# Reordering the tokens while x is split, so that the first product of a fused attention and feed-forward kernel reads plain columns

## The chip, the cores and the metric

The kernel runs on one core of one Trainium2 chip. The metric is the device time of one execution in microseconds; the time of a kernel is the median over several executions. Engines are named as the profile names them: PE is TensorE (PEld its weight loads), DVE is VectorE, ACT is ScalarE, POOL is GpSimd, SP is the engine that issues the DMAs.

## The reference

Windowed attention with 32 global tokens, then a feed-forward block. There are 8 batches with 8 heads, 512 local and 32 global tokens, head size 64; d_model is 512 and d_ff 2048.

```python
s_ll = np.where(abs(i - j) <= 32, scale * q_l @ k_l.T, -1e9)
a_l = softmax(concat[scale * q_l @ k_g.T, s_ll])
out_l = a_l @ concat[v_g, v_l]
out_g = softmax(scale * q_g @ concat[k_g, k_l].T) @ concat[v_g, v_l]
x = concat[out_g, out_l].transpose(0, 2, 1, 3).reshape(4352, 512)
h = x @ w_in
g = h * erf(softplus(h))
return g @ w_out
```

## The kernel before, in words

**Order.** No engine's order is written by hand. Every step is an operation with a key, a guessed duration on each engine that may run it (`add({"DVE": ..., "ACT": ...}, key, ...)`), and the tiles that it reads and writes. `Program.schedule` runs through these guesses once, at build time, and fixes which engine takes which operation and in which order each engine's queue stands. On the chip each queue runs in that order and waits by semaphores. So a changed guess can move other operations too.

**Attention** (`attention`, `attention_global`). For each batch and head: scores `s` (PE), mask and maximum `sm`, `mx` (DVE), exponential (ACT), transposes `t` (PE) copied to `pt`, values `o` (PE), normalised to `xn`, turned to `xT` by a DVE transpose of 32x32 blocks, and stored to a scratch tensor `xsc` in DRAM by four DMAs. The global tokens go the same way through `ga`, `gb`, `pg`, `gt`, `go`, `xg`, `gx` to `xsg`.

**x in DRAM.** Row d of `xsc[b]` holds one feature of 512 tokens. Because the DVE transposes blocks, the tokens of a row stand in the order (a, t, q): a is which of four blocks of 32 within a tile of 128 tokens, t which tile, q the token within the block. Token order would be (t, a, q).

**Feed-forward block.** The 4352 rows of x are nine chunks: eight with 512 local tokens of one batch, and chunk 8 with the 256 global tokens. The weights don't fit at once, so there are two passes (`ps` 0 and 1) over half of d_ff each, and pass 0 leaves its part of the output in DRAM (`part`). Pass 0 is interleaved with the attention of later batches. All products are in fp32r with three terms: a value is split into a high part (`xh`, `winh`, `gh`, `wouth`) and a low part (`xl`, ...), and high·high, low·high and high·low are summed.

- `load_x` loads a chunk's x in two halves `rx` of 128 x 1024 (two slices j of 512 tokens), copies each half to `xh` (which rounds it to fp32r) and subtracts to get `xl`.
- `unit` makes one 128-row slice of h for a chunk: `mm1` issues 4 x 3 = 12 matmuls with `winh` or `winl` as stationary and `xh` or `xl` as moving operand. A chunk of 512 has 8 units in each pass, chunk 8 has 4 of two rows (12 matmuls of 256 columns for each row).
- `gate` computes softplus and erf on ACT, and splits g to `gh`, `gl`.
- `project` issues groups of 6 matmuls `op` (stationary `gh` or `gl`, moving `wouth` or `woutl`, 512 plain columns).

In `mm1` the moving operand of chunks 0 to 7 is read in token order out of the (a, t, q) order:

```python
xh, xl = (t.ap[:, j, :] for t in (HI, LO))
if c < B:
    xh, xl = (t.rearrange("p (a t q) -> p t a q", a=4, q=WB) for t in (xh, xl))
```

That is 16 runs of 32 columns. Chunk 8 reads 256 plain columns. The tiles `xh` and `xl` have three buffers each, so that the second half of the next chunk takes the buffer that the first half of the present one leaves.

Line 278 of the profile is the helper `pe` that records every matmul, 279 the transposes on PE, 280 ACT, 282 DMA, 290 DVE and POOL: groups are told apart by their tiles.

Of the kernel before, what the change touches and what calls it, by code (L numbers as in the profile page):

```python
# [11 lines left out]
F32 = mybir.dt.float32  # L12
# [5 lines left out]
ALU = mybir.AluOpType  # L18
AX = mybir.AxisListType

P = 128
WB = 32
# [23 lines left out]
    "va_0_7": "oh0",  # L46
}
NORMAL = 1.125 * 2.0**-15
SET_EXP = "exp_and_others"
SET_SOFTPLUS = "softplus"  # L50
SET_ERF = "sigmoid_and_others"
# [29 lines left out]
class Program:  # L81
# [9 lines left out]
    def add(self, ways, key, fn, reads=(), writes=(), moved=0.0, heat=0):  # L91


        op = Op()
        op.ways, op.fn, op.key, op.seq, op.moved = ways, fn, key, len(self.ops), moved
        op.heat = heat
        op.outs, op.at, op.new, op.eng = [], 0.0, [], None
        op.slack = max(SLACK.get(e, 0.0) for e in ways)
        op.port = not any(b.pool in self.psum for b in reads)
        deps = set()  # L100
        for b in reads:
            deps.update(b.writers)
        for b in writes:
            deps.update(b.writers)
            deps.update(b.readers)
            if b not in self.allocated:
                self.allocated.add(b)
                if b.pool is not None:
                    op.new.append(b)
        op.bufs = [b for b in dict.fromkeys([*reads, *writes]) if b.pool is not None]  # L110
        for b in op.bufs:
            b.users += 1
        for b in writes:
            b.writers, b.readers = [op], []
        for b in reads:
            if b not in writes:
                b.readers.append(op)
        op.waits = len(deps)
        for d in deps:
            d.outs.append(op)  # L120
        self.ops.append(op)
        return op
# [117 lines left out]
def kernel(  # L240
# [12 lines left out]
    B, NPAIR, _, SQ = qT.shape  # L253
# [22 lines left out]
    add = prog.add  # L276
# [16 lines left out]
    vec = {"DVE": dve, "POOL": pool}  # L293

    def copy(e, dst, src):
        if e == "ACT":
            act(dst, src, AF.Copy)
        else:
            dve.tensor_copy(dst, src)

    def fixed(t):
        b = Buf(None, None, None, None, None)
        b.ap = t
        return b

    def load(key, dst, src, kbytes, deps=(), also=()):
        add({"SP": 0.06}, key, lambda: dma(dst.ap, src), reads=deps, writes=[dst, *also], moved=kbytes)
# [13 lines left out]
    TAB = fixed(None)  # L321
    add({"ACT": 1.3}, -99, lambda: table(SET_EXP), writes=[TAB])

# [256 lines left out]
    def mbuf(shape, dtype, name, tag, bufs):  # L580
        return Buf(mp, shape, dtype, name, tag, bufs)

    def load_w(key, src, name, HI, LO, i, deps):
# [20 lines left out]
        def normal():  # L604
            a = TOP.ap.bitcast(F32)
            dve.scalar_tensor_tensor(
                a, HI.ap[:, i, :].bitcast(F32), NORMAL, a, op0=ALU.is_gt, op1=ALU.mult
            )
# [23 lines left out]
    def load_x(ps, c, key):  # L632

        n = SL if c < B else B * SG
        X = []
        for i in range(2):
            RAW = mbuf([P, 2 * SL], F32, f"rx_{ps}_{c}_{i}", "raw", 3)
            HI = mbuf([P, 2 * SL], F32R, f"xh_{ps}_{c}_{i}", "xh", 3)
            LO = mbuf([P, 2 * SL], F32R, f"xl_{ps}_{c}_{i}", "xl", 3)
            for t in (RAW, HI, LO):  # L640
                t.view = [P, 2, n]
            src = (xsc[c] if c < B else xsg)[2 * P * i : 2 * P * i + 2 * P, :]
            deps = [XSC[c, p] for p in range(2 * i, 2 * i + 2)] if c < B else XSG
            load(key + 0.1 * i, RAW, src.rearrange("(k p) t -> p k t", p=P), 2.048 * n / 2, deps)
            k = key + 0.1 * i + STEP * 2
            add({"DVE": 0.002 * n - 0.2, "ACT": 0.0018 * n + 0.2}, k, lambda e, HI=HI, RAW=RAW: copy(e, HI.ap, RAW.ap), [RAW], [HI])
            add({"POOL": 0.0048 * n + 0.3, "DVE": 0.0026 * n + 0.15},
                k,
                lambda e, HI=HI, LO=LO, RAW=RAW: vec[e].tensor_tensor(
                    LO.ap, RAW.ap, HI.ap.bitcast(F32), ALU.subtract  # L650
                ),
                [RAW, HI],
                [LO],
            )
            X += [(HI, LO, j) for j in range(2)]
        return X

    def unit(ps, c, v, X, key):

        nm = f"{ps}_{c}_{v}"  # L660
        n = SL if c < B else B * SG
        HP = Buf(ps_h, [P, SL // n, n], F32, f"h_{nm}", "h", 2)

        def mm1(a, r):
            o = HP.ap[:, r, :]
            WH, WL = W["in", ps, a // 2]
            for k, (HI, LO, j) in enumerate(X):
                c0 = 256 * (k % 2) + P * (a % 2)
                wh, wl = (t.ap[:, k // 2, c0 : c0 + P] for t in (WH, WL))
                xh, xl = (t.ap[:, j, :] for t in (HI, LO))  # L670
                if c < B:
                    xh, xl = (t.rearrange("p (a t q) -> p t a q", a=4, q=WB) for t in (xh, xl))
                pe(o, wh, xh, start=(k == 0), stop=False)
                pe(o, wh, xl, start=False, stop=False)
                pe(o, wl, xh, start=False, stop=(k == NKT - 1))

        rows = [v] if c < B else [2 * v, 2 * v + 1]
        xs = [t for HI, LO, _ in X[::2] for t in (HI, LO)]
        for r, a in enumerate(rows):
            add({"PE": 0.00533 * n}, key + 0.01 * r, lambda a=a, r=r: mm1(a, r), [*xs, *W["in", ps, a // 2]], [HP], heat=12 * n)  # L680
        Hb = mbuf([P, SL], F32, f"hs_{nm}", "hs", 7)
        SPb = mbuf([P, SL], F32, f"sp_{nm}", "sp", 7)
        add({"ACT": 0.58, "DVE": 0.69}, key, lambda e: copy(e, Hb.ap, HP.ap.rearrange("p a t -> p (a t)")), [HP], [Hb])
        return Hb, SPb

    def gate(ps, c, us, key, first):
        def erf():
# [6 lines left out]
            if ps == 0:  # L694
                table(SET_EXP)

# [109 lines left out]
    for ps in range(2):  # L806
        for c in range(NCHT):
            s = NU * (17 * ps + 2 * c)
            n = NV if c < B else NU
            if ps == 1 and c == 0:  # L810
                for i in range(5, 2 * NU):
                    load_late(i)
            X = load_x(ps, c, s - XLEAD)
            us = [unit(ps, c, v, X, s + v) for v in range(n)]
            last = ps == 1 and c == NCHT - 1
            G = []
            for a, z in ((0, 2), (2, 3), (3, 4)) if last else [(i, i + 4) for i in range(0, n, 4)]:
                G += gate(ps, c, us[a:z], s + z + GOFF, a)
            project(ps, c, G, s + 4 + POFF)
# [76 lines left out]
```

## Time and profile before

| what | value |
|---|---|
| median of 3 runs | 985.0 us (984.0 to 987.04) |
| the profiled execution, its own time | 984.08 us |
| its span on the core, granted PE clock | 982.4 us, 0.988 |
| PE busy | 950.2 us (97%), 9068 matmuls |
| DVE, ACT, POOL busy | 548.2, 540.3, 303.6 us |
| DMA | 127.62 MB, mean 130 GB/s |
| PE share of the chain that ended last | 88% |

The span runs from the first to the last instruction. Busy is the time in which an engine had at least one instruction in flight; matmuls overlap, so the rate of PE is read from the starts of neighbouring matmuls and not from the length of one. The granted clock is 1.00 where the PE ran at 2.4 GHz, and 0.5 where it ran at 1.2 GHz.

### The profile page before, as it was taken

The numbers are of one execution on the slowest core, as the hardware profiler recorded it, in microseconds if no ns is written. First come the engines' busy times: TensorE is split into PE (matmuls) and PEld (weight loads), VectorE is DVE, ScalarE is ACT, GpSimd is POOL, SyncE is SP. The second block draws the span as 40 slices with busy tenths as digits, with TensorE's granted clock in tenths as the row PEclk, the third lists the DMA queues.
The fourth block names the chain that finished last, engine by engine and source line by source line (L and its number), as shares of the span: only waits on it lengthen the run. The fifth ranks groups of instructions, "written<-read, shape, count | busy, mean of one in ns | idle before, by whom it ended". The sixth has DMA issues, their size and how long they took to land.

```text
span 982.4 us, 22140 instructions
## 1 busy us (share of the span) xinstructions
PE 950.2 (97%) x9068; PEld 758.5 (77%) x9068; DVE 548.2 (56%) x1344; ACT 540.3 (55%) x869; POOL 303.6 (31%) x211
## 2 busy tenths in 40 slices
PE   8977899999999999999999999999999999999996
PEld 6756677777778777777888888888888888888895
DVE  5788899584662756855696398323424242333332
ACT  4354586473565645655586756455655544445670
POOL 2232375242342213321153246322213221212140
PEclk9989999999999999999999999999999999999998
DMA  9779876484360662742442334112304040311203
GB/s 356 213 245 288 251 232 189 126 279 121 95 217 0 210 209 61 227 124 82 141 150 65 107 108 129 65 47 83 95 35 129 1 129 0 107 45 43 85 2 107
DMA packets 79740, 127.62 MB, mean 130 GB/s; under 512 B 12184, under 2 KB 37784, under 8 KB 79640
## 3 DMA queue, kind: packets, MB, share of 16 engines
q1 hardware_dynamic: 79640, 126.22, 41.3%
q8 instruction: 71, 1.16, 0.5%
q14 instruction: 29, 0.24, 0.1%
HBM read 99.45 MB, written 26.74 MB: 128 GB/s over the span
## 4 chain that ended last, share of the span: by engine, by line
PE 88%; DVE 7%; DMA 2%; issue 1%; SPq 0%; ACT 0%; DVEq 0%; ACTq 0%
PE op L278 38%; PE h L278 36%; PE s L278 3%; PE o L278 3%; PE t L279 2%; PE spare L278 2%; DVE top_out L290 2%; DVE sm L290 2%; PE go L278 1%; PE ga L278 1%; DMA xsc<-xT 1%; DVE top_in L290 1%; PE gt L279 1%; DVE xT L290 1%; DVE gh L290 0%
## 5 line engine op out<-in xcount | busy, mean ns | idle before, releaser
L278 PE MATMUL h<-xh,winh 128*128 128x512 f32 (+1 forms) x576 | 225.1, 391 | 0.4 <-DVE hs L290 0.4
L278 PE MATMUL h<-xl,winh 128*128 128x512 f32 (+1 forms) x576 | 221.1, 384 | 0.0
L278 PE MATMUL h<-xh,winl 128*128 128x512 f32 (+1 forms) x576 | 221.0, 384 | 0.0
L278 PE MATMUL op<-wouth,gh 128*128 128x512 f32 x544 | 217.3, 399 | 0.5 <-DVE mx L290 0.5
L278 PE MATMUL op<-wouth,gl 128*128 128x512 f32 x544 | 213.2, 392 | 0.0
L278 PE MATMUL op<-woutl,gh 128*128 128x512 f32 x544 | 212.9, 391 | 0.0
L290 POOL TENSOR_TENSOR sp<-sp,hs 128x512 f32<-128x512 f32 x73 | 107.4, 1492 | 212.2 <-ACT sp L280 212.2
L280 ACT ACTIVATE hs<-h 128x512 f32<-128x512 f32 x86 | 51.3, 596 | 162.7 <-PE h L278 162.5
L290 DVE TENSOR_TENSOR gl<-sp,gh 128x512 fp32r<-128x512 f32 x77 | 73.5, 959 | 107.9 <-ACT gh L280 107.0
L280 ACT ACTIVATE gh<-sp 128x512 fp32r<-128x512 f32 x122 | 73.9, 626 | 99.8 <-PE op L278 78.8
L278 PEld LDWEIGHTS h<-xh,winh 128*128 128x128 f32 x576 | 108.7, 189 | 24.9 <-issue 0.8
L278 PEld LDWEIGHTS h<-xh,winl 128*128 128x128 f32 x576 | 108.7, 189 | 23.4
L290 POOL TENSOR_TENSOR gl<-sp,gh 128x512 fp32r<-128x512 f32 x59 | 87.4, 1485 | 126.5 <-ACT gh L280 97.7
L278 PEld LDWEIGHTS h<-xl,winh 128*128 128x128 f32 x576 | 108.8, 189 | 21.5
L278 PEld LDWEIGHTS op<-wouth,gh 128*128 128x128 f32 x544 | 102.2, 188 | 24.1 <-issue 1.7
L278 PEld LDWEIGHTS op<-wouth,gl 128*128 128x128 f32 x544 | 102.1, 188 | 22.1
L278 PEld LDWEIGHTS op<-woutl,gh 128*128 128x128 f32 x544 | 102.3, 188 | 20.6
L281 ACT ACT_TABLE_LOAD x90 | 115.5, 1283 | 2.3 <-PEq L883 0.7
L290 DVE COPY hs<-h 128x512 f32<-128x512 f32 x50 | 34.3, 686 | 108.3 <-PE h L278 108.2
L290 POOL TENSOR_TENSOR sm<-sm,mx 128x512 f32<-128x512 f32 x36 | 40.5, 1130 | 162.8 <-DVE mx L290 98.4
L290 DVE TENSOR_TENSOR sp<-sp,hs 128x512 f32<-128x512 f32 x63 | 65.3, 1058 | 29.9 <-ACT sp L280 29.9
L280 ACT ACTIVATE sp<-sp 128x512 f32<-128x512 f32 x136 | 74.8, 620 | 0.4
(75 smaller groups left out, 1172.5 us busy)
## 6 DMA issues: line engine op xcount, KB each, us to landing
vb<-in_vB_dram SPq DMA_DIRECT2D x64, 325.0 KB, 3.7
rx<-xsc SPq DMA_DIRECT2D x32, 512.0 KB, 4.6
va<-in_vA_dram SPq DMA_DIRECT2D x64, 195.0 KB, 3.6
k<-in_kE_dram SPq DMA_DIRECT2D x32, 384.0 KB, 5.8
q<-in_qT_dram SPq DMA_DIRECT2D x32, 272.0 KB, 4.6
part<-os SPq DMA_DIRECT2D x34, 256.0 KB, 2.1
pr<-part SPq DMA_DIRECT2D x34, 256.0 KB, 3.9
out_dram<-os SPq DMA_DIRECT2D x34, 256.0 KB, 3.9
```

What stands on the lines that cost most here:

```text
L278: pe = lambda n, *a, **k: pinned(nc.tensor.matmul(n, *a, **k))
L279: tr = lambda *a, **k: pinned(nc.tensor.transpose(*a, **k))
L280: act = lambda *a, **k: pinned(nc.scalar.activation(*a, **k))
L281: table = lambda name: pinned(nc.scalar.preload_act_table_set(name))
L290: return lambda *a, **k: pinned(f(*a, **k))
```

## The change

The copy that makes `xh` and the subtraction that makes `xl` now read `rx` in token order and write plain columns. As a half holds two slices j, each of the two operations becomes two instructions of 128 x 512 (chunk 8: 128 x 256, and nothing is reordered there). `mm1` then reads plain columns for every chunk. The guesses for the copy are changed as well. `STRAIGHT` is False, so all of chunks 0 to 7 are reordered.

```diff
-            add({"DVE": 0.002 * n - 0.2, "ACT": 0.0018 * n + 0.2}, k, lambda e, HI=HI, RAW=RAW: copy(e, HI.ap, RAW.ap), [RAW], [HI])
-            add({"POOL": 0.0048 * n + 0.3, "DVE": 0.0026 * n + 0.15},
-                k,
-                lambda e, HI=HI, LO=LO, RAW=RAW: vec[e].tensor_tensor(
-                    LO.ap, RAW.ap, HI.ap.bitcast(F32), ALU.subtract
-                ),
...
+            def in_order(t, j, moved=c < B and not (c == 0 and STRAIGHT)):
+
+                t = t.ap[:, j, :]
+                return t.rearrange("p (a t q) -> p t a q", a=4, q=WB) if moved else t.rearrange("p (t a q) -> p t a q", a=4, t=t.shape[1] // P)
+
+            def split_hi(e, HI=HI, RAW=RAW):
+                for j in range(2):
+                    copy(e, in_order(HI, j, False), in_order(RAW, j))
+
+            def split_lo(e, HI=HI, LO=LO, RAW=RAW):
+                for j in range(2):
+                    hi, lo = (in_order(t, j, False) for t in (HI, LO))
+                    vec[e].tensor_tensor(lo, in_order(RAW, j), hi.bitcast(F32), ALU.subtract)
+
+            add({"DVE": 0.0014 * n, "ACT": 0.0022 * n + 0.1}, k, split_hi, [RAW], [HI])
+            add({"POOL": 0.0048 * n + 0.3, "DVE": 0.0026 * n + 0.15}, k, split_lo, [RAW, HI], [LO])
...
-                xh, xl = (t.ap[:, j, :] for t in (HI, LO))
-                if c < B:
-                    xh, xl = (t.rearrange("p (a t q) -> p t a q", a=4, q=WB) for t in (xh, xl))
+                xh, xl = HI.ap[:, j, :], LO.ap[:, j, :]
```

The number of PE instructions stays what it was. Which engine takes which half moves: before, ACT makes 20 of the 36 `xh` and POOL 16 of the 36 `xl` (DVE the rest); now it is ACT 18 and POOL 20.

DVE, in batch 2's attention, at the second half of x of chunk 0 (names are tile_pass_chunk_half, or tile_batch_head, with a running number). Before:

```order
L290 RECIPROCAL rs_1_5_1698<-rs_1_5_1698 128x4
L290 CAST xh_0_0_1_1707<-rx_0_0_1_1587 128x1024
L290 TENSOR_TENSOR xn_1_4_1589<-o_1_5_1668,rs_1_5_1698 128x4x64
L290 TENSOR_TENSOR xl_0_0_1_1731<-rx_0_0_1_1587,xh_0_0_1_1707 128x1024
L290 STREAM_TRANSPOSE xT_1_5_1747<-xn_1_4_1589 128x512
```

Now:

```order
L291 RECIPROCAL rs_1_5_1700<-rs_1_5_1700 128x4
L291 CAST xh_0_0_1_1709<-rx_0_0_1_1589 128x512 x2
L291 TENSOR_TENSOR xn_1_4_1591<-o_1_5_1670,rs_1_5_1700 128x4x64
L291 TENSOR_TENSOR xl_0_0_1_1734<-rx_0_0_1_1589,xh_0_0_1_1709 128x512 x2
L291 STREAM_TRANSPOSE xT_1_5_1751<-xn_1_4_1591 128x512
```

Nothing moved here; each of the two operations became two instructions.

PE, further on in the attention of batch 2, at the first place at which its order differs. Before (of the eight rows of scores `s_2_4` the last two stand here, of the twelve of unit `h_0_0_3` the first):

```order
L278 MATMUL s_2_4_0_1995<-k_2_4_1753,q_2_4_1751 32x128 x4
L278 MATMUL s_2_4_1_1996<-k_2_4_1753,q_2_4_1751 32x128 x4
L279 MATMUL t_2_2_2050<-cs_75,sm_2_2_1905 128x128 x4
L279 MATMUL t_2_3_2059<-cs_75,sm_2_3_1912 128x128 x4
L278 MATMUL h_0_0_3_2068<-xh_0_0_0_1050,winh_0_1_142 128x512
```

Now (again the last two rows of the `s_2_4`, and the first of `s_2_6`, of `o_2_2` and of `h_0_0_3`):

```order
L280 MATMUL t_2_2_2008<-cs_75,sm_2_2_1906 128x128 x4
...
L279 MATMUL s_2_4_0_2026<-k_2_4_1757,q_2_4_1755 32x128 x4
L279 MATMUL s_2_4_1_2027<-k_2_4_1757,q_2_4_1755 32x128 x4
L279 MATMUL gx_2_0_2068<-cs_75,xg_2_0_2024 128x64
L280 MATMUL t_2_3_2071<-cs_75,sm_2_3_1917 128x128 x4
L279 MATMUL s_2_6_0_2079<-k_2_6_1761,q_2_6_1759 32x128 x4
...
L279 MATMUL o_2_2_2118<-va_2_2_1698,pt_2_2_2009 32x65
...
L279 MATMUL h_0_0_3_2135<-xh_0_0_0_1050,winh_0_1_142 128x512
```

The transposes `t_2_2` moved ahead of the scores, `gx_2_0` ahead of `t_2_3`, and unit `h_0_0_3` behind `s_2_6` and the first values `o_2_2`. From here to the end of attention PE's order differs in many places. Counted over the whole program, PE's order changed from attention work to an `h` or `op` product 90 times before and 83 times now, and an `op` group followed an `h` of a chunk of 512 directly 52 times before and 50 times now.

## Rows read from the trace of the kernel before

**Rows 1.** Busy time by stretch, whole core: us, busy (count) by engine, clock, DMA.

```profile
89.50:166.50 77.00, 70.41 (x1162) 54.69 (x1158) 71.94 (x226) 50.41 (x97) 40.06 (x28) 0.98 0.79 245
166.50:973.10 806.60, 806.59 (x6220) 647.55 (x6220) 410.41 (x864) 450.33 (x692) 237.91 (x159) 1.00 0.34 104
```

**Rows 2.** The same stretches, instructions that touch tile h alone (no POOL column).

```profile
89.50:166.50 77.00, 37.57 (x144) 26.93 (x144) 2.70 (x4) 4.53 (x8) 0.98 0.79 245
166.50:973.10 806.60, 363.85 (x1584) 283.56 (x1584) 31.58 (x46) 46.76 (x79) 1.00 0.34 104
```

**Rows 3.** Waits of PE, 89.5 to 166.5 and behind: us, times, longest.

```profile
PE t L279 <- DVE xg L290: 4.2, 1, 4.2
...
PE op L278 <- DVE mx L290: 0.5, 1, 0.5
```

**Rows 4.** The chain that ended last, pieces: start us, us, what.

```profile
698.92 5.48 PE op L278 x24
...
712.68 8.40 PE h L278 x36
...
935.76 7.19 PE h L278 x60
```

**Rows 5.** Timeline of PE, 700 to 712: start us, us of one, instruction.

```profile
702.88 0.39 PE L278 MATMUL op<-wouth,gh 128*128 128x512 f32 x1
...
704.24 0.40 PE L278 MATMUL h<-xh,winh 128*128 128x512 f32 x1
...
707.03 0.39 PE L278 MATMUL op<-wouth,gh 128*128 128x512 f32 x1
...
708.42 0.39 PE L278 MATMUL op<-wouth,gh 128*128 128x512 f32 x1
```

**Rows 6.** Groups by form on PE: count, busy us, mean ns, idle before.

```profile
L278 PE MATMUL h<-xh,winl 128*128 128x256 f32 x64 | 18.1, 283 | 0.0
```

**Rows 7.** Tile xh: engine, operation, count, ns min/median/max, first and last start, forms.

```profile
L280 ACT ACTIVATE xh<-rx x20: 623/1058/1064, 52.3 to 927.5; 128x1024 fp32r<-128x1024 f32 x18, 128x512 fp32r<-128x512 f32 x2
L290 DVE TENSOR_TENSOR xl<-rx,xh x20: 682/1218/2322, 88.1 to 930.1; 128x1024 fp32r<-128x1024 f32 x19, 128x512 fp32r<-128x512 f32 x1
L290 POOL TENSOR_TENSOR xl<-rx,xh x16: 1288/2393/3252, 54.0 to 886.3; 128x1024 fp32r<-128x1024 f32 x13, 128x512 fp32r<-128x512 f32 x3
L290 DVE CAST xh<-rx x16: 417/694/1604, 87.2 to 885.8; 128x1024 fp32r<-128x1024 f32 x14, 128x512 fp32r<-128x512 f32 x2
```

**Rows 8.** Timeline of DVE, 84 to 130, two instructions.

```profile
88.08 1.22 DVE L290 TENSOR_TENSOR xl<-rx,xh 128x1024 fp32r<-128x1024 f32 x1
...
106.14 2.34 DVE L290 TENSOR_SCALAR gh<-cs,gr 128x2 f32<-128x2 f32 x1
```

**Rows 9.** Timelines of POOL and of PE, around 106 us; in brackets the idle time before.

```profile
106.12 2.34 POOL L290 TENSOR_TENSOR xl<-rx,xh 128x1024 fp32r<-128x1024 f32 x1 [1.69 <-ACT xh L280]
...
108.95 1.09 PE L279 MATMUL t<-cs,sm 128*128 128x128 f32 x4 [4.21 <-DVE xg L290]
```

**Rows 10.** Timeline of PE around one group of attention work between two h units.

```profile
226.10 0.40 PE L278 MATMUL h<-xh,winl 128*128 128x512 f32 x1
226.43 0.24 PE L278 MATMUL o<-va,pt 128*32 128x65 f32 x1
...
227.47 0.50 PE L278 MATMUL h<-xh,winh 128*128 128x512 f32 x1
227.81 0.40 PE L278 MATMUL h<-xl,winh 128*128 128x512 f32 x1
```

**Rows 11.** Timelines of ACT, POOL and PE at the change of chunk in pass 1.

```profile
750.15 1.06 ACT L280 ACTIVATE xh<-rx 128x1024 fp32r<-128x1024 f32 x1 [1.61 <-PE h L278]
...
751.29 2.40 POOL L290 TENSOR_TENSOR xl<-rx,xh 128x1024 fp32r<-128x1024 f32 x1 [10.57 <-ACT xh L280]
...
756.84 0.40 PE L278 MATMUL h<-xh,winh 128*128 128x512 f32 x1
```

**Rows 12.** The chain that ended last, 85 to 200 us: the longest piece that isn't PE's.

```profile
94.69 5.67 DMA xsc<-xT
```

More of the change, by code (lines that the diff above doesn't have):

```diff
@@ L48 @@
 NORMAL = 1.125 * 2.0**-15
+STRAIGHT = False
 SET_EXP = "exp_and_others"
@@ L645, in load_x @@
             k = key + 0.1 * i + STEP * 2
-            add({"DVE": 0.002 * n - 0.2, "ACT": 0.0018 * n + 0.2}, k, lambda e, HI=HI, RAW=RAW: copy(e, HI.ap, RAW.ap), [RAW], [HI])
-            add({"POOL": 0.0048 * n + 0.3, "DVE": 0.0026 * n + 0.15},
-                k,
-                lambda e, HI=HI, LO=LO, RAW=RAW: vec[e].tensor_tensor(
-                    LO.ap, RAW.ap, HI.ap.bitcast(F32), ALU.subtract
-                ),
-                [RAW, HI],
-                [LO],
-            )
+            def in_order(t, j, moved=c < B and not (c == 0 and STRAIGHT)):
[10 more added lines that the diff above has]
+            add({"POOL": 0.0048 * n + 0.3, "DVE": 0.0026 * n + 0.15}, k, split_lo, [RAW, HI], [LO])
             X += [(HI, LO, j) for j in range(2)]
```

## The prediction

> **What bounds the kernel now.** I read the busy time by stretch first. Between 166.5 and 973.1 us PE has work in flight for 806.59 of 806.60 us at a clock of 1.00 (2.4 GHz) [rows 1]. The list of PE's waits agrees: behind 89.5 us it has one long wait, 4.2 us for `xg`, and the last one, 0.5 us, ends the early stage [rows 3]. So from 166.5 us on the end is set by how fast PE goes through its queue, and by nothing else: a nanosecond taken from a matmul there is a nanosecond off the time. Ahead of it, from 89.5 to 166.5 us, DVE is the fuller engine (71.94 of 77 us busy, PE 70.41 [rows 1]); there PE's gain can be lost in waits for DVE. Ahead of 89.5 us no `h` product runs.
>
> Then I read PE's rate, from the starts of matmuls and not from their lengths. In the chain, 36 `h` matmuls of 512 columns take 8.40 us, 0.2333 us each, and 24 `op` matmuls of the same size 5.48 us, 0.2283 us each [rows 4]. The timeline splits the `op` number. The six `op` ahead of an `h` unit take 704.24 − 702.88 = 1.36 us, 0.2267 us each; the six right behind an `h` unit take 708.42 − 707.03 = 1.39 us [rows 5]. The reader is to see two things: the steady gap is 6.7 ns a matmul, and the first groups of `op` behind `h` lose about 0.04 us (5.48 − 4 x 1.36, for four groups of six).
>
> Is the gap due to the order of the columns, or to something else in `h`, its tiles, its weights, its PSUM buffers? Chunk 8 is the control: same code, same pools, but 256 plain columns, 7.19 us for 60, 0.1198 us each [rows 4]. At 2.4 GHz, 256 columns are 0.1067 us and 512 are 0.2133 us. What a matmul takes beyond its columns is then 13.1 ns for plain `h`, 13.4 ns for plain `op`, and 20.0 ns for reordered `h`. The extra goes with the order: 6.7 ns is 16 periods of 2.4 GHz, and the pattern has 16 runs.
>
> **The change part by part.**
>
> *The 512-column `h` matmuls (A).* Behind 166.5 us there are 1584 `h` matmuls [rows 2], of which 3 x 64 = 192 have 256 columns [rows 6]: 1392 x 6.67 ns = 9.3 us. Between 89.5 and 166.5 us there are 144 [rows 2], worth 0.96 us. PE waits for DVE there, so I count half, 0.5 us; the bounds are 0 and 0.96.
>
> *The slow `op` behind `h` (B).* If `h` streams at the rate of `op`, the change of rate is gone, and 52 x 0.04 = 2.1 us with it. Nothing in the trace shows a plain 512-column `h` ahead of `op`, so the bounds are 0 and 2.1 us. I take 2.1, since within a run of `op` a change of group costs nothing.
>
> *Groups of attention work between products (C).* The reshuffled order has 83 of them where there were 90. One costs 227.81 − 227.47 − 0.23 = 0.11 us on the way back to `h`, and 226.43 − 226.10 − 0.23 = 0.10 us on the way out [rows 10]. Seven fewer are worth 0.7 (one way) to 1.5 us; I take 1.1 us.
>
> *The split on the early path (D).* The first `h` can start only when the DVE's `xl` of 88.08 us, 1.22 us long, is done [rows 8]. In two instructions of 512 it takes 2 x 0.682 = 1.36 us, and the copy 2 x 0.417 = 0.83 in place of 0.694 us [rows 7]: +0.3 us, all counted. The trace has no DVE copy with a reordered source. If it ran at the pace of the subtraction (0.682 us for 512) it would add 0.5 us more. It can't be less than nothing: there are as many elements and more instructions. I take 0.3, as the pattern only breaks into 16 runs. The Trainium skill (VectorE: DVE Perf Modes, Mode 2×_2P) lets an fp32 copy in SBUF keep two elements per cycle when the outermost dimension is even, here 4; no row here shows it for this pattern, and by it D would be the 0.3 taken.
>
> *The splits behind 166.5 us.* Two instructions cost more on every engine: ACT 1.06 to 2 x 0.623 = 1.25 us, POOL 2.39 to 2 x 1.288 = 2.58 us [rows 7]. What hides them is that PE has other work. The tightest place is the second half of a chunk: its `xh` waits for a buffer that the present chunk leaves, at 750.15 us; its `xl` is done at 751.29 + 2.40 = 753.69, and `h` reads it from 756.84 [rows 11]. The margin is 3.15 us, and 0.4 us of it goes. Cost: nothing. Without the cover it would be 0.4 us for each of 16 chunks, 6.4 us in all.
>
> *The early order (E).* Around 104.7 us PE waits 4.2 us: `xg` stands on DVE behind a 128x2 operation that took 2.34 us, and this ended together with a POOL subtraction of `xl` that began at the same time and took as long [rows 8, 9]. In the new order `gx_2_0`, `t_2_3`, `s_2_6` and part of `o_2_2` stand ahead of `h_0_0_3` on PE, so less product work can start early behind that wait; on the other hand the POOL operation is now two halves, and the DVE may get in between. The place can gain the whole stall or get a second one. A stall's price is 4.2 us plus the lower clock behind it, (1 − 0.98) x 77 = 1.5 us [rows 1]: 5.7 us. I take 0 and keep ±5.7 for the range.
>
> **Sum.** The profiled execution took 984.1 us, its span 982.4. 984.1 − 9.3 − 0.5 − 2.1 − 1.1 + 0.3 = 971.4 us. It was 0.9 us below the median of 985.0, so for a median I say **972.3 us**. No change that can be measured is within 0.3%, 982.0 to 988.0 us.
>
> **The rivals.**
>
> 1. *Plain columns are no faster for `h`.* The 0.2333 us would belong to something that `h` has at 512 columns alone. Against it stands chunk 8's 13.1 ns beyond its columns; for it, that no 512-column plain `h` is in the trace. A and B fall: 984.1 − 1.1 + 0.3 + 0.9 = 984.2 us, no change. It decides if the starts of `h` stay 0.233 us apart. Two pages speak for it. The Trainium skill (SBUF — State Buffer, Door 1: The DMA port swizzle) has reads lose only where they go to a new line of 16 bytes, and runs of 32 fp32 go to as many lines as plain columns do; and (TensorE: Matmul & The Clock Gate, Step-by-step: what each phase is for) it takes one column of the moving operand per cycle whatever the pattern. By these rules the reordered read was free all along. The trace disagrees so far: 20.0 against 13.4 ns.
>
> 2. *One more early stall.* The mechanism of E comes out on the bad side once: 972.3 + 5.7 = 978.0 us, still faster. For it speaks that DVE is 93% busy from 89.5 to 166.5 us [rows 1] and gets longer instructions; against it, that the assignment in the first chunk is unchanged.
>
> 3. *Slower: DVE's queue blocks on the store of `xT`.* `xT` has one buffer, and a transpose had to wait for a store that held the chain for 5.67 us [rows 12]; what PE needs next then stands behind it in DVE's queue. The new order moves these transposes among other work. Each time that PE has nothing else meanwhile costs about 5.7 us, by the same account as a stall in E. With 12.7 us gained and 3.0 us to be seen, it takes three such places between 105 and 420 us: 972.3 + 17.1 = 989.4 us. Against it: PE has not one such wait behind 166.5 us now, with DVE busy for half of the time there (410.41 of 806.60 us [rows 1]).
>
> **Chances.** Forecast 0.80, rival 1 0.08, rival 2 0.07, rival 3 0.05. So faster by over 0.3%: 0.87, within 0.3%: 0.08, slower: 0.05. The range: the low end is the forecast with the present stall gone, 972.3 − 5.7, about 967. The high end is rival 2 with B at zero, 978.0 + 2.1, about 980. That leaves out rivals 1 and 3 and the ends of the others, under 2 in 10.
>
> **What would show it.** In the profile after: starts of `h` matmuls 0.227 us apart in pass 1, and a chain with 36 of them in about 8.16 us; 24 `op` behind `h` in 5.44 us in place of 5.48; PE busy without a gap from about 165 us to its last matmul; `xl` on POOL in pieces of 1.3 us, and of 0.68 us on DVE; the idle time of PE between 90 and 166 us still about 6.6 us. The prediction is wrong if `h` keeps 0.233 us, if the list of PE's waits has new entries of several microseconds, or if the `xl` of a chunk's second half ends after the first `h` of that chunk could start.

## The result, and the profile after

The change made the kernel faster: a median of 976.3 us (973.44 to 977.58, 5 runs) against 984.0 us (981.61 to 987.04, 5 runs) for the kernel before. The ratio is 0.9917, with a 95% interval of 0.989 to 0.9945, which is −8.1 us. The forecast was 972.3 us in a range of 967 to 980. The profiled execution took 973.44 us, the fastest of the five, with a span of 971.6 us at a granted clock of 0.988.

The rate of PE first. These are pieces of the chain that ended last, of the changed kernel (start us, us, what); they answer to [rows 4].

```profile
725.05 5.44 PE op L279 x24
...
749.53 8.16 PE h L279 x36
...
925.08 7.19 PE h L279 x60
```

36 `h` now take 8.16 us, 0.2267 us each, and the 24 `op` behind an `h` unit take 5.44 us, so the gap in rate and the slow first `op` are both gone. Chunk 8, which was not touched, keeps its 7.19 us.

Then the busy time by stretch (us, then busy us and count for PE, PEld, DVE, ACT and POOL, then clock and DMA), which answers to [rows 1]:

```profile
88.00:165.00 77.00, 70.29 (x1147) 54.19 (x1140) 74.71 (x225) 49.20 (x96) 38.97 (x29) 1.00 0.73 232
165.00:962.50 797.50, 794.43 (x6249) 647.55 (x6247) 413.84 (x907) 448.43 (x700) 243.28 (x175) 1.00 0.35 107
```

and PE's waits behind 165 us (what waited, for what; us in all, times, longest), which answer to the end of [rows 3]:

```profile
PE s L279 <- issue: 1.3, 1, 1.3
PE gx L279 <- DVE xg L291: 0.8, 1, 0.8
PE t L280 <- ACT os L281: 0.8, 1, 0.8
```

The products stage, in windows set behind an early stage of 77 us each, is 9.1 us shorter, 797.50 for 806.60 us, with 29 more matmuls in it; but it is not solid any more. It lacks 797.50 − 794.43 = 3.07 us of PE, where it lacked 0.01 us before [rows 1], and three waits of the attention work among the products hold 2.9 us of that. In the early stage the wait of 4.2 us for `xg` has become several smaller ones:

```profile
PE t L280 <- ACT pg L281: 1.9, 1, 1.9
PE t L280 <- DVE gt L291: 1.0, 1, 1.0
PE gx L279 <- DVE xg L291: 0.9, 1, 0.9
```

The split itself, by the tile `xh` (engine, operation, count, ns of the shortest, median and longest; answers to [rows 7]):

```profile
L291 POOL TENSOR_TENSOR xl<-rx,xh x40: 737/1294/1811, 52.8 to 877.5; 128x512 fp32r<-128x512 f32 x34, 128x256 fp32r<-128x256 f32 x6
L281 ACT ACTIVATE xh<-rx x36: 402/617/634, 51.1 to 917.2; 128x512 fp32r<-128x512 f32 x32, 128x256 fp32r<-128x256 f32 x4
L291 DVE CAST xh<-rx x36: 285/420/1520, 86.3 to 876.1; 128x512 fp32r<-128x512 f32 x32, 128x256 fp32r<-128x256 f32 x4
L291 DVE TENSOR_TENSOR xl<-rx,xh x32: 414/680/1781, 87.2 to 919.8; 128x512 fp32r<-128x512 f32 x30, 128x256 fp32r<-128x256 f32 x2
```

For 128x512 with a reordered source the medians are 617 ns on ACT, 1294 on POOL, 680 (subtraction) and 420 (copy) on DVE. Plain ones of that size took 623, 1288, 682 and 417 ns at the least [rows 7]. So the reordered source costs nothing that these rows show. The Trainium skill (VectorE: DVE Perf Modes, Mode 2×_2P) lets an fp32 copy in SBUF keep two elements per cycle for this pattern; the 420 ns agree, as a plain copy took 417.

### The profile page after: what moved, and what is told of

Its sections match the earlier page's. It is cut to its first block, busy times and chain, and to the rows that moved or that the text cites. A ratio compares the mean times of both kernels' runs of the same rounds, so it can differ in the third digit from the quotient of the medians.

```text
span 971.6 us, 22208 instructions
## 1 busy us (share of the span) xinstructions
PE 937.7 (97%) x9068; PEld 757.9 (78%) x9068; DVE 553.7 (57%) x1386; ACT 537.8 (55%) x876; POOL 308.3 (32%) x230
## 4 chain that ended last, share of the span: by engine, by line
PE 87%; DVE 6%; DMA 4%; issue 1%; ACT 1%; SPq 0%; DVEq 0%; ACTq 0%
PE op L279 38%; PE h L279 35%; PE o L279 3%; PE s L279 3%; PE t L280 2%; PE spare L279 2%; DVE top_out L291 2%; PE ga L279 1%; DMA rx<-xsc 1%; PE go L279 1%; DMA xsc<-xT 1%; PE gt L280 1%; DVE top_in L291 1%; DVE sm L291 1%; DMA part<-os 1%
## 5 line engine op out<-in xcount | busy, mean ns | idle before, releaser
L279 PE MATMUL h<-xh,winh 128*128 128x512 f32 (+1 forms) x576 | 221.1, 384 | 0.0
L279 PE MATMUL h<-xh,winl 128*128 128x512 f32 (+1 forms) x576 | 217.8, 378 | 0.0
L279 PE MATMUL h<-xl,winh 128*128 128x512 f32 (+1 forms) x576 | 217.6, 378 | 0.0
L291 DVE TENSOR_TENSOR gl<-sp,gh 128x512 fp32r<-128x512 f32 x77 | 70.4, 918 | 109.1 <-ACT gh L281 108.7
L281 ACT ACTIVATE hs<-h 128x512 f32<-128x512 f32 x82 | 48.9, 597 | 137.6 <-PE h L279 137.4
L291 POOL TENSOR_TENSOR gl<-sp,gh 128x512 fp32r<-128x512 f32 x59 | 86.1, 1464 | 112.9 <-ACT gh L281 90.6
L291 DVE COPY hs<-h 128x512 f32<-128x512 f32 x54 | 37.1, 686 | 110.8 <-PE h L279 110.6
L291 POOL TENSOR_TENSOR xl<-rx,xh 128x512 fp32r<-128x512 f32 (+1 forms) x40 | 52.3, 1328 | 119.4 <-ACT xh L281 72.8
L291 POOL TENSOR_TENSOR sm<-sm,mx 128x512 f32<-128x512 f32 x34 | 38.3, 1130 | 139.4 <-DVE mx L291 95.9
L291 DVE TENSOR_TENSOR sp<-sp,hs 128x512 f32<-128x512 f32 x63 | 61.0, 986 | 31.6 <-ACT sp L281 31.5
```

Source lines behind the costliest of these rows:

```text
L279: pe = lambda n, *a, **k: pinned(nc.tensor.matmul(n, *a, **k))
L281: act = lambda *a, **k: pinned(nc.scalar.activation(*a, **k))
L291: return lambda *a, **k: pinned(f(*a, **k))
```

## The experiments

What was to be found out: the forecast was 4 us low and its sum has four parts. The first four kernels take the change apart, the next two follow what that showed, and the last four ask what else the order of the columns can give. A ratio is always to the kernel before, run beside it on the same chip.

### The change with the engine order of before

```diff
-            add({"DVE": 0.0014 * n, "ACT": 0.0022 * n + 0.1}, k, split_hi, [RAW], [HI])
+            add({"DVE": 0.002 * n - 0.2, "ACT": 0.0018 * n + 0.2}, k, split_hi, [RAW], [HI])
```

> The change with the old guesses for the copy, so that every engine's order and every assignment is that of the kernel before; only the reordered split in two pieces and the plain read of the first product are new. Theory: the matmul rate is worth about 11.9 us (9.3 + 0.5 + 2.1) and what is missing in the whole change went to the new order; then this kernel takes 984.0 - 11.9 + 0.3 = 972.4 us, ratio 0.988, and PE shows no wait over 0.5 us behind 170 us. Rival: the reordered split itself costs the missing microseconds; then this kernel is no better than the change, about 976 us, ratio 0.992.

Measured: 972.24 us (970.71 to 972.83), ratio 0.9882 (0.9861 to 0.9903). The change of order that comes with the new guesses is therefore not a gain: without it the kernel is 0.0035 x 984 = 3.4 us faster than the change as it stands, though the two intervals overlap at their ends. In this trace PE has none of the three waits that the change has behind 165 us, and the busy times of the stretch show PE solid again:

```profile
165.30:961.30 796.00, 795.93 (x6218) 646.66 (x6216) 414.66 (x898) 451.44 (x705) 239.57 (x171) 1.00 0.35 105
```

### The order alone

The kernel before, with the new guesses and nothing else.

```diff
-            add({"DVE": 0.002 * n - 0.2, "ACT": 0.0018 * n + 0.2}, k, lambda e, HI=HI, RAW=RAW: copy(e, HI.ap, RAW.ap), [RAW], [HI])
+            add({"DVE": 0.0014 * n, "ACT": 0.0022 * n + 0.1}, k, lambda e, HI=HI, RAW=RAW: copy(e, HI.ap, RAW.ap), [RAW], [HI])
```

> The kernel before with the new guesses for the copy alone: new order and new assignment, but the old split and the old reordered read. Theory: the new order takes back some microseconds, 986 to 988 us, with waits of PE of about 1 us near 200, 215 and 350 us. Rival, the prediction's term C: seven groups of attention work fewer are worth 1.1 us, 983 us.

Measured: 986.58 us (982.53 to 990.45, 12 runs), ratio 1.003 (1.0014 to 1.0045), so about 3 us slower. It confirms the reading of the first experiment from the other side. PE's waits behind 170 us show a price of the same kind as in the change:

```profile
PE s L278 <- issue: 1.8, 1, 1.8
PE ga L278 <- ACT os L280: 1.1, 1, 1.1
PE t L279 <- ACT os L280: 0.6, 1, 0.6
```

Behind the first of these, which ended at 218.67 us, the granted clock was 0.50 (1.2 GHz) from 219.5 to 222.9 us, and six `op` there took 2.54 us in place of 1.36. Neither the kernel before nor the change has such a stretch between 165 us and the end of the products, so this profile lost more to the new order than that of the change.

What ACT and DVE stood for is in their own lists of waits, 165 to 475 us. Of the change:

```profile
DVE xh L291 <- DMA rx<-xsc: 2.0, 1, 2.0
...
ACT os L281 <- DMA part<-os: 5.8, 3, 3.1
```

Of the order alone:

```profile
DVE xh L290 <- DMA rx<-xsc: 1.3, 2, 0.9
...
ACT os L280 <- DMA part<-os: 6.6, 3, 4.3
```

Before, the second of these entries stood at 0.4 us and the first was not in the list; in the change with the old order neither is in the list. So in the new order DVE comes to a copy of x before its load has landed, and ACT to an `os` whose buffer is still being stored, and the attention's operations that stand behind these in the two queues come late for PE. The timeline of DVE shows one case in the change:

```profile
346.27 0.76 DVE L291 CAST xh<-rx 128x512 fp32r<-128x512 f32 x2 [1.96 <-DMA rx<-xsc]
346.95 0.28 DVE L291 TENSOR_TENSOR xg<-go,gh 128x128 f32<-128x128 f32 x1
```

`xg` starts only behind the copy, and PE's `gx` has its wait of 0.8 us for this `xg`.

### The plain read alone

The kernel before, with the reordering taken out of `mm1` and not put anywhere else, so its output rows stand in the order (a, t, q).

```diff
-                if c < B:
-                    xh, xl = (t.rearrange("p (a t q) -> p t a q", a=4, q=WB) for t in (xh, xl))
```

> The kernel before, old order and old split in one piece, but the first product reads plain columns; the reordering is left out altogether, so that the tokens of a chunk come out in the order (a, t, q). Theory: this is the gain of the read alone, 984.0 - 11.9 = 972.1 us, with starts of h 0.2267 us apart and no slow op behind h. Rival, the slow op behind h stay (term B is nothing): 974.2 us. If the split in two reordered pieces is hidden, e1_old_order takes the same time within 0.5 us.

Measured: 974.12 us (973.33 to 975.22), ratio 0.9906 (0.9888 to 0.9925), −9.3 us with an interval of −7.4 to −11.0. The chain has 36 `h` in 8.16 us here too. So the rate is a matter of the columns' order alone, and reading plain columns is worth 9 us and not the 11.9 us of A and B.

The time is that of the rival, by which the slow `op` stay, but the trace is against it. Added up over the starts from the 144th `h` on, the intervals that begin with a 512-column `h` are 329.3 us before and 321.2 here, 8.2 less where A had 9.3; those that begin with `op` are 369.2 and 367.2, 2.1 less, as B had it. PE idles 1.0 us there in this execution, which takes a part of it back. The change with the old order, which also has the two pieces, is 1.9 us faster and not within 0.5 us, which leads to the next kernel.

### The two pieces alone

The kernel before, with its permuted read, its guesses and its plain copies, but each copy and each subtraction of `xh` and `xl` in two pieces of 512 columns.

```diff
+            def split_hi(e, HI=HI, RAW=RAW):
+                for j in range(2):
+                    copy(e, in_order(HI, j, False), in_order(RAW, j))
...
-            def in_order(t, j, moved=c < B and not (c == 0 and STRAIGHT)):
+            def in_order(t, j, moved=False):
```

> The kernel before, old order, with each copy and subtraction of x in two plain pieces of 512; the first product still reads the reordered columns. Theory: only the 0.3 us ahead of the first h shows, 984.3 us, no difference that can be measured. Rival: the longer pieces delay DVE and POOL in the early stage by more than a stall, 987 us or more.

Measured: 981.05 us (978.37 to 984.98, 12 runs), ratio 0.997 (0.9952 to 0.9989): a gain of 3.0 us where the prediction had a loss of 0.3. Since nothing reads faster in this kernel, the gain comes from the pieces. The place to look is the wait of 4.2 us [rows 8, 9]. Timelines of this kernel there (start us, us, instruction; in brackets the idle time before and who ended it):

```profile
104.60 2.50 POOL L291 TENSOR_TENSOR xl<-rx,xh 128x512 fp32r<-128x512 f32 x2 [1.26 <-ACT xh L281]
...
105.05 0.84 DVE L291 TENSOR_SCALAR gh<-cs,gr 128x2 f32<-128x2 f32 x1
...
106.36 0.63 PE L280 MATMUL t<-cs,sm 128*128 128x128 f32 x4 [2.13 <-DVE xg L291]
```

DVE's small `gh` ends at 105.89 us. The first of POOL's two pieces (1.27 us) ends at 105.87. Before, the one piece ended at 108.46 and `gh` at 108.48 [rows 8, 9]. So DVE seems to be let go when POOL's instruction ends, and a shorter one lets it go sooner. The next two kernels test this.

### Pieces on POOL alone, two and four

First the kernel before, in which only POOL's `xl` is in two pieces and every DVE and ACT instruction is as it was:

```diff
-                lambda e, HI=HI, LO=LO, RAW=RAW: vec[e].tensor_tensor(
-                    LO.ap, RAW.ap, HI.ap.bitcast(F32), ALU.subtract
-                ),
+                lambda e, HI=HI, LO=LO, RAW=RAW: [
+                    vec[e].tensor_tensor(LO.ap[:, j, :], RAW.ap[:, j, :], HI.ap[:, j, :].bitcast(F32), ALU.subtract)
+                    for j in range(2)
+                ] if e == "POOL" else vec[e].tensor_tensor(LO.ap, RAW.ap, HI.ap.bitcast(F32), ALU.subtract),
```

> The kernel before, old order, old copies and old reordered read; only the subtractions that POOL does are in two pieces of 512. Theory: POOL holds the 128x2 operation of DVE for one piece in place of two (0.84 us in place of 2.34 us), the wait of PE behind it shrinks from 4.2 to 2 or 3 us, and the time falls as it did with all splits in two pieces: 981 to 982.6 us, ratio about 0.997. Rival: the gain came from the two copies, or it is noise; then 984.1 us, ratio 1.000.

Then the change with the old guesses, and POOL's `xl` in four pieces of 256:

```diff
-                    vec[e].tensor_tensor(lo, in_order(RAW, j), hi.bitcast(F32), ALU.subtract)
+                    raw, hi = in_order(RAW, j), hi.bitcast(F32)
+                    n = lo.shape[1]
+                    for s in [slice(m, m + n // 2) for m in (0, n // 2)] if e == "POOL" else [slice(0, n)]:
+                        vec[e].tensor_tensor(lo[:, s], raw[:, s], hi[:, s], ALU.subtract)
```

> The change with the old guesses and order, and the subtractions of POOL in four pieces of 256. Theory: the 128x2 operation of DVE is held for at most 0.7 us and PE's wait shrinks by some tenths of a microsecond more; 971.5 us, ratio about 0.987, and no kernel so far is faster. Rival: more pieces on POOL delay the low parts and open a wait of PE elsewhere; 973 us or more.

Measured: two pieces on POOL alone 979.93 us (978.57 to 984.73, 12 runs), ratio 0.9967 (0.9951 to 0.9983). That is the whole gain of the two pieces on all engines. Four pieces with the plain read 968.49 us (968.04 to 972.14, 4 runs), ratio 0.9845 (0.9825 to 0.9864), where two pieces stood at 0.9882 (0.9861 to 0.9903); as the two intervals touch, a further gain by four pieces is likely and not shown. The timelines at the same place, of the first kernel and then of the second:

```profile
103.36 2.49 POOL L290 TENSOR_TENSOR xl<-rx,xh 128x512 fp32r<-128x512 f32 x2 [1.69 <-ACT xh L280]
...
103.39 1.26 DVE L290 TENSOR_SCALAR gh<-cs,gr 128x2 f32<-128x2 f32 x1
...
104.89 0.41 DVE L290 TENSOR_TENSOR xn<-o,rs 128x256 f32<-128x256 f32 x1
...
105.12 0.63 PE L279 MATMUL t<-cs,sm 128*128 128x128 f32 x4 [3.23 <-DVE xg L290]
```

```profile
105.69 3.28 POOL L291 TENSOR_TENSOR xl<-rx,xh 128x256 fp32r<-128x256 f32 x4 [1.26 <-ACT xh L281]
...
106.14 0.30 DVE L291 TENSOR_SCALAR gh<-cs,gr 128x2 f32<-128x2 f32 x1
...
106.91 1.09 PE L280 MATMUL t<-cs,sm 128*128 128x128 f32 x4 [2.24 <-DVE xg L291]
```

The 128x2 operation takes 2.34 us beside a POOL instruction of 2.34 us, 1.26 beside a piece of 1.26 (0.84 was expected, but it began with the piece), and 0.30 beside a piece of 0.73 (the first of the four) that had begun 0.45 us ahead of it. In all eleven traces in which it overlaps POOL's `xl` it ends 0.02 to 0.03 us behind the POOL instruction that runs. So DVE is held to the end of that instruction, and not only at this place. In the kernel before, three other operations of DVE ahead of 166 us end 0.3 or 0.5 us behind an `xl` of POOL and last far longer than elsewhere (0.4, 0.7 and 0.4 us): 2.05 us at 54.5 us, 2.60 at 141.2, 1.84 at 161.1. With two pieces on all engines the same three take 0.97, 1.76 and 0.75 us. Not every operation is held: `xn` above runs beside POOL's second piece in 0.41 us, as it does elsewhere with POOL idle.

Over their shortest time in any trace, the operations that `xl` holds ahead of 170 us last, added up, 7.2 us longer in the kernel before, 5.5 and 5.1 with two pieces (POOL alone, all engines), since a second piece holds the next operation, and 2.2 with four. How much of this reaches the end is less sure. PE's wait for `xg` falls from 4.2 to 3.2 and 2.2 us here, but it was 3.4 us in the plain read alone, where POOL's `xl` is in one piece. From the first `h` to the 144th, the kernels in one piece that read x as before in pass 0 (the kernel before and the two of the next two sections) take 84.6 to 86.0 us, and those in two pieces 83.1 and 83.9. About 2 of the 3 us can be seen there; the rest was not separated.

### How long must a run be?

The kernel before, in which chunk after chunk of pass 1 reads x in two interleaved stretches with runs of 256, 128, 64, 16, 8, 4, 2 and 1 columns.

```diff
+                    r = (256, 128, 64, 16, 8, 4, 2, 1)[c] if ps == 1 else WB
...
+                    elif r == 1:
+                        xh, xl = (t.rearrange("p (k m) -> p m k", k=2) for t in (xh, xl))
+                    else:
+                        xh, xl = (t.rearrange("p (k m q) -> p m k q", k=2, q=r) for t in (xh, xl))
```

> The kernel before, old order; in pass 1 each chunk's first product reads the 512 columns of x in another order (so the values of pass 1 belong to other tokens): 2 runs of 256 in chunk 0, then runs of 128, 64, 16, 8, 4, 2 and single columns in chunks 1 to 7. Pass 0 keeps 16 runs of 32. Theory, one period of 2.4 GHz for each run: the starts of h are 0.2267 us and 2, 4, 8, 32, 64, 128, 256 and 512 periods apart, that is 0.2275, 0.2283, 0.230, 0.240, 0.2533, 0.280, 0.333 and 0.440 us. Rival, the rule of 16-byte lines (the Trainium skill, SBUF - State Buffer, Door 1: The DMA port swizzle): runs of 4 columns and more are free, so chunks 0 to 5 stand at 0.2267 us, and only runs of 2 and 1 are slower. A third way, a cost for any reordered read whatever the length of its runs: 0.2333 us in all eight.

One run, 993.93 us, read by the chain. One piece of 24 `h` for each chunk of pass 1, in the order of the list:

```profile
594.00 5.44 PE h L278 x24
...
637.52 5.44 PE h L278 x24
...
681.04 5.44 PE h L278 x24
...
725.09 5.76 PE h L278 x24
...
770.15 5.84 PE h L278 x24
...
815.59 6.01 PE h L278 x24
...
864.77 8.15 PE h L278 x24
...
904.17 5.18 PE h L278 x24
```

That is 0.2267 us for a matmul with runs of 64 and more, then 0.240 (16), 0.243 (8), 0.250 (4) and 0.340 (2), and 0.2158 us for single columns from the two halves in turn. All theories failed. One period for each run, which had fitted the 16 runs of 32 (16 periods) and fits the 32 runs of 16 (0.2400 − 0.2267 = 13.3 ns, 32 periods), would give 26.7 ns for runs of 8, and these cost 16.7. The rule of 16-byte lines (the Trainium skill, SBUF — State Buffer, Door 1: The DMA port swizzle) would let all runs of 4 and more go free, and runs of 32, 16, 8 and 4 all cost something. What sets the cost stays open. And the last chunk is faster than plain columns, which no theory had.

### More than two stretches, and columns apart

The kernel before again; pass 1 reads single columns in turn from 4, 8, 16 and 32 stretches (chunks 0 to 3), every 2nd, 4th and 16th column (4 to 6), and runs of 32 from the two halves (7).

```diff
+                    elif c < 4:
+                        xh, xl = (t.rearrange("p (k m) -> p m k", k=(4, 8, 16, 32)[c]) for t in (xh, xl))
+                    elif c < 7:
+                        xh, xl = (t.rearrange("p (m k) -> p k m", k=(2, 4, 16)[c - 4]) for t in (xh, xl))
+                    else:
+                        xh, xl = (t.rearrange("p (k m q) -> p m k q", k=2, q=32) for t in (xh, xl))
```

> The kernel before, old order; in pass 1 each chunk's first product reads its 512 columns in another pattern (the values of pass 1 belong to other tokens): one column in turn from each of 4, 8, 16 and 32 equal stretches in chunks 0 to 3; every 2nd, every 4th and every 16th column in chunks 4 to 6; in chunk 7 runs of 32 in turn from two halves. It asks what the run of single columns in turn from two halves (0.216 us, faster than plain columns at 0.2267 us) rests on. Theory: what costs is staying in one place; any number of stretches read in turn by single columns stands at 0.216 us, strided reads of one stretch do not, and runs of 32 stand at 0.2333 us as in the kernel before, 16 periods over plain. Rival: 0.216 us belongs to two stretches alone, and more of them, or steps between columns that go to a new 16-byte line each time, are slower than plain, up to 0.340 us as the runs of two columns were.

One run, 1112.19 us. The chain gave these pieces of 24 `h`, for chunks 0 to 7:

```profile
593.90 6.77 PE h L278 x24
...
633.09 11.77 PE h L278 x24
...
717.26 10.44 PE h L278 x24
...
780.75 10.40 PE h L278 x24
...
844.86 10.87 PE h L278 x24
...
910.47 11.04 PE h L278 x24
...
975.58 10.40 PE h L278 x24
...
1020.75 5.68 PE h L278 x24
```

0.282, 0.490, 0.435, 0.433, 0.453, 0.460, 0.433 and 0.237 us for a matmul. The theory that any number of stretches read in turn gives 0.216 us fell, and so did the rival's upper end of 0.340 us. The gain belongs to the two halves read column by column; of the patterns tried none other has it. Every 16th column is the same order as one column in turn from each of 32 stretches, so the two 0.433 us are a repeat, and every 2nd and every 4th column are 256 and 128 stretches in turn. The 16 runs of 32 from two halves cost 0.237 us, where those of the kernel before, taken from four blocks, cost 0.2333: neither the length nor the number of the runs sets the cost alone.

### The two halves as a version of the kernel

The kernel with four pieces on POOL, in which `mm1` reads the two halves in turn; the rows of the output are stored to where the tokens of that order belong.

```diff
+                if c < B:
+                    xh, xl = (t.rearrange("p (k m) -> p m k", k=2) for t in (xh, xl))
...
-            n = c * SQ + SG + t * P
-            return out[n : n + P, :]
+            n = c * SQ + SG
+            return out[n : n + 4 * P, :].rearrange("(k t m) d -> t m k d", k=2, t=4)[t]
```

> e7_pool_four_pieces (old order, POOL in four pieces), but the first product of chunks 0 to 7 takes one column in turn from the two halves of the token order, and the last DMA writes the output rows back to their places, so that the result is the reference's. Theory: this read stands at 0.2158 us a matmul as in e5_run_lengths, 10.9 ns under plain; 1536 matmuls are worth 16.7 us, and the time is 968.5 - 16.7 = 951.8 us, ratio 0.967. Rival: the rate is lost to the slow matmuls at each change of rate between h and op, some 0.04 us or more at each of 110 changes; then 956 us or more.

And the same with `op` reading `wouth` and `woutl` that way too, whose columns lie in two halves in DRAM for it:

```diff
+                wh, wl = (w.ap[:, a, :].rearrange("p (k m) -> p m k", k=2) for w in (WH, WL))
...
-    wo = np.ascontiguousarray(moe_w_out).view(np.int64).reshape(2, 4, 2, P, 512)
+    wo = np.ascontiguousarray(moe_w_out).view(np.int64).reshape(2, 4, 2, P, 256, 2)
+    wo = np.ascontiguousarray(wo.swapaxes(-1, -2)).reshape(2, 4, 2, P, 512)
```

> e9_two_halves, and the second product reads its moving operand in the same way; the columns of w_out are laid out in the matching order ahead of the launch, so the result is the reference's. Theory: 1632 more matmuls at 0.2158 us, 17.8 us less, 951.8 - 17.8 = 934.0 us, ratio 0.949, with h and op at one rate. Rival: the rate belongs to the tiles of x and not to the pattern; then op stays at 0.2267 us and the time at 952 us.

Measured: `h` alone 956.1 us (953.89 to 959.04), ratio 0.9723 (0.9698 to 0.9748); both products 939.79 us (937.42 to 942.26), ratio 0.9555 (0.9528 to 0.9582). Both gain less than was expected (951.8 and 934.0 us), the first as much as its rival had it (956 us). The second product gains as the first did, so the rate belongs to the pattern and not to the tiles of x. The chain of the first, then of the second:

```profile
821.17 7.77 PE h L279 x36
828.94 5.47 PE op L279 x24
```

```profile
728.02 7.77 PE h L279 x36
735.79 5.18 PE op L279 x24
740.97 5.18 PE h L279 x24
```

With two rates in turn the slow first `op` behind `h` are back (5.47 for 5.44 us); with one order, 0.2158 us for both, they are gone again. It is plain `op` behind `h` in another order that loses; `h` behind `op`, a change of rate too, runs at its 0.2158 us from its first starts. By the starts from the 144th `h` on, `h` gains 15.3 us in the first kernel over the one with four pieces, all that was expected of the 1392 there, and `op` loses 1.1 us, so the rival's mechanism accounts for that much. Where the rest of the missing 4 us lies stays open: the profiled executions of the two kernels are 972.14 − 956.1 = 16.0 us apart. What is missing in the second kernel is in part a new entry in PE's list of waits behind 170 us, for DVE's `hs` of the gate:

```profile
PE h L279 <- DVE hs L291: 3.3, 2, 1.8
```

## Why the prediction was right, and where it was not

**What bounds the kernel.** Right. Taking time from the matmuls behind 166.5 us took it from the end, in every kernel that did it.

**A and B, the faster `h` and the slow `op` (9.3 + 0.5 + 2.1 = 11.9 us).** The mechanism was right, and its signs are there: `h` at 0.2267 us, 36 in 8.16 us, 24 `op` in 5.44 us. B had the right size too, 2.1 us by the starts. The size of A was off, 8.2 us for 9.3. The read alone measured 9.3 us (7.4 to 11.0), and the change with the order of before against the two pieces alone 0.9882 / 0.997 = 0.9912, 8.7 us. A part of the difference can be pointed at. Behind a group of attention work plain `h` does not run at 0.2267 us at once, and neither does `op`. Starts in the change with the old order (start us, us, instruction):

```profile
225.76 0.40 PE L279 MATMUL h<-xl,winh 128*128 128x512 f32 x1
...
227.82 0.39 PE L279 MATMUL h<-xl,winh 128*128 128x512 f32 x1
```

Nine starts from 225.76 to 227.82 us are 0.2289 us each. At the same unit the kernel before had its usual 0.233 right behind the entry. So there the gain is 4 to 5 ns and not 6.7 for about ten matmuls, at 27 such entries behind 175 us about 0.9 us by a count over all their starts, which lose more on the mean. The prediction's step that failed was to take the rate in the middle of the products for all 1392 matmuls. About 1.0 us more is what PE idles in the plain read alone, and the rest of the 11.9 us is less than the interval of the measurement leaves open.

**C, the order (−1.1 us).** Wrong in its sign. Fewer changes between attention work and products were priced by what one change takes [rows 10]; what was not priced is what stands ahead of the attention's operations in DVE's and ACT's queues in the new order. The order alone costs 3 us (an interval of 1.4 to 4.4), and the waits that go with it are on PE for ACT's `os` and DVE's `xg`, behind a load and a store, and, in the middle of a group of scores, for nothing that the profile shows ("issue"; 1.3 us in the change, 1.8 in the order alone). What that last one is stays open. The sign asked for, PE without a gap from 165 us on, failed by these 3 us.

**D, the two pieces (+0.3 us).** Wrong in its sign: they gain 3 us. "It can't be less than nothing: there are as many elements and more instructions" was the step that failed. The price of an instruction is also what it does to the neighbour that must wait for its end; [rows 8, 9] had the fact, a DVE operation that ended with POOL's, and E even named the halves on POOL as a chance, but left it at zero. The pace of the reordered copy was right, 420 ns.

**E, the early stage (0 within 5.7 us).** The stall of 4.2 us went and smaller ones came (1.9, 1.0, 0.9 us). In this execution DVE's 128x2 operation starts at 104.23 us, 0.21 us ahead of POOL's first piece, and takes 0.23 us, so it was not held; in the order alone it starts 0.04 us ahead of POOL and is held for 2.40 us. The clock between 88 and 165 us was 1.00 in this execution. The start of the first `h` differs from run to run by up to 4 us (86.5 to 90.6 us over the profiled kernels with the order of before), so one profile says little about a term of this size.

**The splits behind 166.5 us (nothing).** Right: among PE's waits behind 165 us there is none for `xh` or `xl`.

**The sum.** Read −9.3, pieces −3.0, order +3.0 make −9.3 us; the change measured −8.1 us, with an interval of −5.4 to −10.8. Against the terms, A and B were 2.6 us too large, C 4.1 us too favourable and D 3.3 us too dear. The errors of C and D nearly cancel, so it is luck that the time came out within the range with two of its terms wrong in sign.

**The rivals.** The first, that plain columns are no faster, fell by the starts of `h`. The second, one more early stall, did not come as such: the early waits became smaller, and what the new order lost it lost behind 165 us. The third has a grain of what happened: DVE's wait for the store of `xT` did not grow (2.2 us before, 0.8 in the change, 165 to 475 us), but a queue that blocks on a DMA ahead of PE's work is how the order lost a part of its 3 us (1.6 of the 2.9 us of waits in the change), with the load of x and the store of the partial output in that store's place. The two rules of the Trainium skill behind the first rival (SBUF — State Buffer, Door 1: The DMA port swizzle; TensorE: Matmul & The Clock Gate, Step-by-step: what each phase is for) would have made the read free. The runs disagree: 0.2333 against 0.2267 us for the same columns, and from 0.2158 to 0.490 us over all orders tried.

## What to carry to other kernels

Where PE has no gap, read the distance of matmul starts and look at the access pattern of the moving operand: here the order alone moved a matmul of 512 columns between 0.216 and 0.49 us. Where a guess in a scheduler changes with an edit, time the edit with the old order as well: here the better edit and the worse order came in one diff, and the old order was worth 3 us. And an instruction on one engine can be worth splitting for the sake of another engine that waits for its end: `xl` of POOL in two pieces, and nothing else, was worth 0.33%.

## What the runs showed of the hardware

- Two halves of 512 columns, read column by column in turn, gave a matmul each 0.2158 us (24 in 5.18 us). Plain columns gave 0.2267 us, although the chip ran at the same clock of 1.00. That made the fastest kernel here, at 939.79 us. The window of its products stage shows PE busy for 757.86 of 761.50 us:

```profile
170.00:931.50 761.50, 757.86 (x6175) 647.65 (x6173) 412.68 (x893) 448.94 (x701) 242.26 (x194) 1.00 0.36 110
```

- Beyond that the cost of a pattern rose in no simple way: runs of 64 and more like plain columns, 16 and 8 nearly alike (0.240 and 0.243 us), 2 at 0.340, and single columns from 8 stretches (0.490) worse than from 32 (0.433).
- A DVE operation of 128x2 elements took 2.34, 1.26, 0.84 or 0.30 us, according to what was left of the POOL instruction beside it, and ended 0.02 to 0.03 us behind it. Other operations of DVE were held too, and some, as `xn`, were not.
- Plain-column matmuls, `h` or `op`, ran some 4 ns slower on the mean for about ten starts behind attention work (2 ns at the place shown), and plain `op` lost about 40 ns at each entry behind `h` in the order of the kernel before. `h` in that order and products read from two halves in turn showed no such slow starts; why, no run here shows.
